# A staged copy issued ahead of a turn instead of behind it, in a depthwise convolution fused with a two-layer network

## The chip, the cores and the metric

The kernel runs on one core of a Trainium2 chip. The core has five engines, each with an instruction queue of its own that it works through in order: TensorE (PE) multiplies matrices into PSUM, VectorE (DVE), ScalarE (ACT) and GpSimd (POOL) work on tiles, and SyncE (SP) here does nothing but start DMAs and pass signals on. Engines wait for each other by semaphores. The metric is the device time of one execution in microseconds (us).

## The reference

Each head h has seven weights, made by a softmax over `weight`. The input `x` (8 sequences of 4096 tokens, 192 channels in 8 heads of 24) is convolved along the sequence with them, and the result goes through two products with a gate between:

```
w = softmax(weight, axis=-1)                      # 8 heads x 7 taps
c[b, s, h, g] = sum_k w[h, k] * x[b, s - 6 + k, h, g]   # zero before a sequence
hid = c @ w_in                                    # 192 -> 2048
y = (hid * cos(hid)) @ w_out                      # 2048 -> 192
```

There are 32,768 tokens. Inputs and output are float32; the kernel multiplies in bfloat16.

## The kernel before

**Tiles and units.** The two products go tile by tile, 512 tokens each, 64 tiles in all. The convolution goes unit by unit, 1024 tokens each, so a unit feeds two tiles: an even one and an odd one. While tiles of unit u are multiplied, the convolved and transposed input of unit u+1 is made ready in a buffer `cT`, of which there are two.

**How a unit is made.** From the fourth unit on (`FIRST_RAW`), part of the tokens is convolved by PE with a band matrix (`conv_unit`, matmuls of L284) and part by ACT and POOL tap by tap on a transposed copy `rT`. Both parts meet in a staging tile `ro`: the first part comes there by two DMA transposes (`turn_unit`, L326), the second by the last of POOL's three additions (`sum_raw`, L393, L394, L396). Then `spread_raw` issues four DMAs from SP that copy the staging tile to both halves of `cT` (L408, L409, twice each). The change is about these four.

**Products.** Product 1 (`mm1`, L524) makes `h` from `cT`, eight steps of a tile, called h0 to h7, each six matmuls; ACT takes its cosine (L531), DVE multiplies (L535). Product 2 (`mm2_step`, L573) uses the `g` of an earlier tile and takes 128 matmuls a tile, in 64 steps of two. The two matmuls of a step work on two halves of PE's rows and write to two banks.

**The turns.** Half way through a tile's product 2 the two row halves change banks. So that no two of them write one bank at once, `Turn` puts an empty instruction on SP (L203) that waits for the last matmuls of the first half (`mark`); the first matmuls of the second half wait for that instruction (`wait`). `conv_unit` has a turn of the same kind between its first eight and its last eight matmuls. So PE goes on past a turn only once SP has come to that empty instruction, and SP comes to it only when it is done with everything that it was given before.

**Order of work.** It is written out by hand as strings. In `PE_ORDER`, one string for even and one for odd tiles, `mN` is N steps of product 2, `hJ` a step of product 1, `q` marks the place of product 2's turn (its empty instruction has been given to SP with the last step ahead of `q`), `c1` and `c2` are the two halves of `conv_unit`, with its turn between. Letters with a number are work on a unit that many ahead: `S` sum_raw, `X` and `x` the transposes to the staging tile, `K` a cast, `R` tap_raw (four multiplications on POOL, L386), `T` the transpose to `rT` (L353), `L` loads, `U` spread_raw; `O` stores results, `p` marks the end of product 2 of a tile. Where an item stands in the string is where its instructions stand in their own engine's queue; an item for SP takes no place on PE. `PE_FIRST` has the strings of the first six tiles.

In the odd tile SP is given: the empty instruction of product 2's turn, the four copies (U+1), the empty instruction of the convolution's turn (c1), the transpose T+3, a store, three loads. In the even tile: the turn of product 2, two transposes X+1 and x+1, a store.

Of the kernel before, what the change touches and what calls it, by code (L numbers as in the profile page):

```python
# [16 lines left out]
def kernel(  # L17
# [14 lines left out]
    T = 512  # L32
# [87 lines left out]
    wo_src = moe_w_out.rearrange("(i j p) d -> p j i d", i=2, p=128)  # L120

    def cast_wo(q):
        have.add(("wo", q))
        nc.gpsimd.tensor_copy(out=wo[:, q * QP : (q + 1) * QP], in_=wo_f[:, q * QP : (q + 1) * QP])  # L124

# [88 lines left out]
    def cast_unit(u, n0=0, n1=UB + 1, copy=nc.gpsimd.tensor_copy):  # L214
        if u >= FIRST_RAW:
            xk[u] = xk_pool.tile([128, NC * (UB + 1), 64], BF16, name="xk")
            for n0, n1 in ((NPB, UB + 1), (0, NPB)):
                copy(out=xk[u][:, NC * n0 : NC * n1].rearrange("p (k n) m -> p k n m", k=NC),  # L218
                     in_=x_tiles[u][:, n0:n1].rearrange("p n (m k) -> p k n m", k=NC))
            if u % UPS == 0:  # L220
                nc.gpsimd.memset(xk[u][0 : 128 - OP, 0 : NC * NPB : NPB], 0.0)
            return
        if n0 == 0:
            bf[u] = xb0 if u == 0 else xbf_pool.tile([128, UB + 1, D], BF16, name="x_bf")
        o = 1 if u == 0 else 0
        copy(out=bf[u][:, n0 + o : n1 + o, :].rearrange("p n (h k r) -> p (n h) k r", k=NC, r=R),  # L226
             in_=x_tiles[u][:, n0:n1, :].rearrange("p n (h r k) -> p (n h) k r", k=NC, r=R))
# [27 lines left out]
    def conv_part(u, c, banks, whole=False):  # L255


        ps = banks()
        nb = UB + 1
        for i in range(4):  # L260
            conv_mm(u, c, ps, i, slice(0, 128), 0, nb, start=i % 2 == 0, stop=i % 2 == 1)
        if u == 1 and c == 0:
            spread_taps(ps[1][:, nb * 2 * G : nb * 2 * G + K])
        yield
        yield
        if u not in ct_tiles:
            ct_tiles[u] = ct_pool.tile([128, UB + 1, NC, 2, 64], BF16, name="ct")
        for b in range(2):
            conv_out(u, c, ps, 0, 0, nb, copies[by[0]], banks=(b,))
            if b and u == 1 and c == 0:  # L270
                nc.scalar.copy(tap, ps[1][:, nb * 2 * G : nb * 2 * G + K])
            if b:
                have.add(("conv", u, c))
            yield

    def conv_unit(u, banks):


        ps = banks()
        sides = [slice(0, 64), slice(64, 128)]  # L280

        def mm(h, side):
            first, last = h % 4 == 0 and h // 4 == side, h % 4 == 3 and h // 4 != side
            return nc.tensor.matmul(  # L284
                out=ps[h // 4][:, 0 : NPB * 4 * G].rearrange("p (m i r) -> p i m r", m=NC * NPB, i=4)[:, h % 4],
                lhsT=band[sides[side], h, 128 - OP : 256 - OP], rhs=xk[u][sides[side], 0 : NC * NPB, R * h : R * (h + 1)],
                start=first, stop=last, skip_group_check=True)

        for h in range(4):
            ms = mm(h, 0), mm(h + 4, 1)  # L290
        turn = Turn()
        turn.mark(*ms)
        yield
        for h in range(4):
            ms = mm(h + 4, 0), mm(h, 1)
            if h == 0:
                turn.wait(*ms)
        yield
        both = ps[0].tensor, ps[0].offset, [ps[0].ap[0][0], OP]
        for n0, n1 in ((1, NPB), (0, 1)):  # L300
            to = ct_bufs[u % 2][0:OP, 2 * NC * min(n0, 1) : 2 * NC * (min(n0, 1) + 1)]
            to = to.rearrange("p (k n) (b w) -> p b k n w", k=NC, b=2)[:, :, :, 0 : n1 - n0]
            nc.scalar.copy(to, bass.AP(both[0], both[1] + 4 * R * n0, [both[2], [T, 2], [NPB * 4 * R, NC], [4 * R, n1 - n0], [1, 4 * R]]))  # L303
            if n0 == 0:
                have.update((("conv", u, 0), ("conv", u, 1)))
            yield
# [75 lines left out]
    def tap_raw(u):  # L382

        p = raw_prod
        for j in range(NG):
            nc.gpsimd.tensor_scalar(out=p[:, j], in0=tap_window(u, PA + j), scalar1=tap[:, PA + j : PA + j + 1],  # L386
                                    scalar2=1.0, op0=ALU.mult, op1=ALU.mult)

    def sum_raw(u):

        assert {("tap", u, j, PARTS[k].start) for j in range(PA) for k in "lr"} <= have
        a, p, add = pa.pop(u), raw_prod, nc.gpsimd.tensor_tensor
        add(out=p[:, 0:PA], in0=p[:, 0:PA], in1=a, op=ALU.add)  # L393
        add(out=p[:, 0:2], in0=p[:, 0:2], in1=p[:, 2:4], op=ALU.add)  # L394
        have.add(("summed", u))
        add(out=stage_of(u)[:, :, NLO * OP : LO], in0=p[:, 0].rearrange("p (k w) t -> p k (w t)", k=NC),  # L396
            in1=p[:, 1].rearrange("p (k w) t -> p k (w t)", k=NC), op=ALU.add)
# [29 lines left out]

    tc.add_manual_dep(nc.sync.nop().ins, summed.ins.name, sync_dep, reason="order of the transfers")
    LOADS = "b l r e | 0 1 2 3"
    for k in LOADS.split("|")[0].split():  # L430
        loads[k]()

    three = {"D": nc.vector.tensor_copy, "A": nc.scalar.copy, "P": nc.gpsimd.tensor_copy}
    for i, k in enumerate("DPDPDPDPDPDPDPAA"):
# [12 lines left out]
    def conv_first():  # L447

        banks = o_banks()
        for half in range(2):  # L450
            for h in range(H):
                for prev in range(2):
                    nc.tensor.matmul(
                        out=banks[half][:, 0 : 2 * D].rearrange("p (n k h r) -> p h n k r", n=2, k=NC, h=H)[:, h],
                        lhsT=band[:, h, 128 * prev : 128 * prev + 128],
                        rhs=bf[0][:, 2 * half + 1 - prev : 2 * half + 3 - prev, h * G : (h + 1) * G].rearrange(
                            "p n (k r) -> p n k r", k=NC),
                        start=(h == 0 and prev == 0), stop=(h == H - 1 and prev == 1), skip_group_check=True)
            m = copies[half](out=ct_tiles[0][:, 2 * half : 2 * half + 2].rearrange("p n k t w -> p (n k) t w"),  # L459
                             in_=banks[half][:, 0 : 2 * D].rearrange("p (m t w) -> p m t w", t=1, w=64).to_broadcast(  # L460
                                 [128, 2 * NC, 2, 64]))
        tc.add_manual_dep(nc.sync.nop().ins, m.ins.name, sync_dep, reason="order of the transfers")
        for k in LOADS.split("|")[1].split():
            loads[k]()

    def turn_first(half):
        for n in range(2):
# [130 lines left out]
    def finish(t):  # L598
        o_sb[t] = opool.tile([128, NB, D], FP32, name="o_sb")
        for si in range(2):  # L600
            for b in range(2):
# [5 lines left out]

    PE_ORDER = ['m11 h0 m3 h1 S+1 m6 h2 m8 q X+1 h3 K+3 m6 h4 m17 h5 x+1 m9 O p h6 h7 m4', 'm11 h0 m5 h1 R+2 m7 h2 m5 q U+1 h3 m8 h4 m6 c1 m12 c2 T+3 h5 m6 O p L+4 h6 h7 m4']  # L610
    ACT_ORDER = ['s0 s1 s2 a0l2 s3 s4 Q a1l4 a1r4 V s5 s6 s7', 'a0r0 s0 s1 s2 s3 a2l3 s4 a2r4 ec1 Q ec2 s5 P s6 s7']

    PE_FIRST = ["K1 k1 h0a h0b W0 W1 h1 h2 h3 r h4 w5 d11 w4 h5 d21 W2 W3 c11 X0 m1 h6 m11 h7 L2 c21 D1",
# [5 lines left out]
    ACT_FIRST = ["s0a s0b s1 s2 er er s3 s4 ed11 ed21 s5 ec11 s6 ec21 s7",  # L619
                "s0 s1 s2 s3 s4 s5 ec12 ec22 Q P s6 ed12 s7 ed22",  # L620
                "s0 s1 s2 s3 Q s4 P s5 s6 s7",
# [11 lines left out]
    for t in range(NT + 1):  # L633
# [34 lines left out]

        def of_unit(k, v):
            if (k, v) == ("K", 1):  # L670
                cast_unit(1, 0, NB)
            elif (k, v) == ("k", 1):
                cast_unit(1, NB)
            elif k == "Z":
                nc.gpsimd.memset(ct_bufs[v][0:OP, 0 : 2 * NC], 0.0)
            elif (k, v) == ("X", 0):
                turn_unit(0, NB, UB)
            elif k == "L":
                load_unit(v)
                if v < FIRST_RAW:  # L680
                    load_edges(v)
            else:
                {"K": cast_unit, "D": double_unit, "X": turn_unit, "Y": mend_edges, "T": turn_raw, "R": tap_raw, "B": more_taps, "S": sum_raw,
                 "U": spread_raw, "x": lambda u: turn_unit(u, part=1)}[k](v)

        for k in pe.split():
# [13 lines left out]
                made = step // (2 * STEPS) - 1  # L700
            elif k == "q":
                assert step % (2 * STEPS) == STEPS
            elif k[0] == "W":
                cast_wo(int(k[1]))
            elif k == "O":
                while stored <= made and (stored, 0) in evacs and (stored, 1) in evacs:
                    store(stored)
                    stored += 1
            elif k[1:] and k[1] != "+":
                of_unit(k[0], int(k[1]))  # L710
            else:
                if u + int(k[2:]) < NU and (k[0] not in "RSUx" or u + int(k[2:]) >= FIRST_RAW):
                    of_unit(k[0], u + int(k[2:]))
# [35 lines left out]
```

## Time and profile before

| | |
|---|---|
| median of three executions | 702.14 us (702.13 to 702.61) |
| the profiled execution's own time | 702.85 us |
| its span, first to last instruction | 700.9 us |
| granted TensorE clock | 0.999 |
| busy share of PE, DVE, ACT, POOL | 99%, 93%, 92%, 82% |

The span leaves out 1.95 us around the instructions. The chain of waits follows the work that ended last back through what released it. In the timeline, a DMA instruction's time is the time that SP is held by it, not that of the transfer. The waits view lists for each engine and line what ended its idle time. PE's weight loads are listed as PEld, beside PE.

### The profile page before, as it was taken

The page shows a single profiled execution, that of the slowest core. Times are in us where ns is not written, and L with a number is a line of the kernel's source. Part 1 is how long each engine was busy: PE and PEld are TensorE (multiplying, and loading weights), DVE is VectorE, ACT ScalarE, POOL GpSimd, SP SyncE. Part 2 cuts the span into 40 slices and gives each one's busy share as a digit, 9 for nine tenths or more (in the row PEclk, how much of TensorE's full clock was granted, in tenths as well). Part 3 has the DMA queues.
Part 4 walks back from the last instruction along what each step waited for, and adds up shares of the span by engine and source line. Part 5 has one row for each costly group of instructions (what it writes and reads, how often), then busy time and mean ns, then how long its engine had stood idle before and what let it go on. Part 6 is the DMA issues. An engine that isn't in the chain of part 4 may idle for free.

```text
span 700.9 us, 26910 instructions
## 1 busy us (share of the span) xinstructions
PE 693.0 (99%) x11838; PEld 505.5 (72%) x11838; DVE 651.1 (93%) x628; ACT 643.4 (92%) x799; POOL 577.3 (82%) x309
## 2 busy tenths in 40 slices
PE   8999999999999999999999999999999999999998
PEld 4677777777776777777777767777777777777776
DVE  6899999999999999999999999999999999999996
ACT  7889999999999999999999999999999999999875
POOL 6698888899888898888898888988888988887600
PEclk9999999999999999999999999999999999999999
DMA  8992666546765457665556654577654466653232
GB/s 211 204 212 70 147 147 142 106 138 148 169 144 124 115 129 170 152 152 94 146 137 169 146 134 110 128 162 162 149 125 117 126 169 161 146 105 84 68 92 69
DMA packets 163133, 95.99 MB, mean 137 GB/s; under 512 B 68808, under 2 KB 162632, under 8 KB 163016
## 3 DMA queue, kind: packets, MB, share of 16 engines
q1 hardware_dynamic: 162304, 93.30, 57.5%
q8 instruction: 92, 1.51, 0.9%
q0 software_dynamic: 416, 0.79, 0.8%
q14 instruction: 25, 0.20, 0.1%
q10 hardware_dynamic: 296, 0.20, 0.1%
HBM read 31.36 MB, written 25.17 MB: 81 GB/s over the span
## 4 chain that ended last, share of the span: by engine, by line
PE 94%; SPq 2%; DVE 1%; ACT 1%; issue 0%; POOL 0%; POOLq 0%
PE h L524 46%; PE o_ps L573 46%; PE h L284 1%; SPq L409 1%; SPq L408 1%; DVE g L535 1%; ACT cs L531 1%; PE h L573 0%; DVE band L436 0%; ACT ct L493 0%; POOL mask L166 0%; PE h L236 0%; ACT mask L171 0%; ACT ct L459 0%; DVE diag L426 0%
## 5 line engine op out<-in xcount | busy, mean ns | idle before, releaser
L535 DVE TENSOR_TENSOR g<-h,cs 128x1024 bf16<-128x1024 f32 (+1 forms) x513 | 597.3, 1217 | 20.7 <-ACT cs L531 12.2
L531 ACT ACTIVATE cs<-h 128x1024 bf16<-128x1024 f32 (+1 forms) x513 | 510.6, 1022 | 45.0 <-PE h L524 37.3
L573 PEld LDWEIGHTS <-g 64*128 64x128 bf16 x8192 | 353.5, 94 | 102.0 <-issue 0.4
L573 PE MATMUL o_ps<-wo,g 64*128 64x192 bf16 x8128 | 413.3, 243 | 0.0
L524 PE MATMUL h<-cT,w 64*128 64x512 bf16 (+1 forms) x3078 | 405.5, 376 | 1.0 <-DVE g L535 0.6
L393 POOL TENSOR_TENSOR raw_prod<-raw_prod,pa 128x3105 f32<-128x3105 f32 x29 | 164.7, 5679 | 64.4 <-ACT pa L377 64.4
L524 PEld LDWEIGHTS <-w 64*128 64x128 bf16 x3078 | 142.9, 94 | 77.6 <-issue 2.4
L386 POOL TENSOR_SCALAR raw_prod<-rT,tap 128x1035 f32<-128x1035 bf16 x116 | 130.5, 1150 | 0.6 <-DMA rT<-xk 0.5
L377 ACT ACTIVATE pa<-rT,tap 128x575 f32<-128x575 bf16 (+1 forms) x168 | 119.0, 728 | 0.0
L394 POOL TENSOR_TENSOR raw_prod<-raw_prod 128x2070 f32<-128x2070 f32 x29 | 111.6, 3847 | 2.3
L218 POOL CAST xk<-x_f 128x1152 bf16<-128x1152 f32 (+1 forms) x58 | 77.8, 1374 | 1.6 <-DMA x_f<-in_x_dram 1.6
L396 POOL TENSOR_TENSOR ro<-raw_prod 128x1035 bf16<-128x1035 f32 x29 | 69.1, 2381 | 2.3
L592 DVE COPY o_sb<-o_ps 128x384 f32<-128x384 f32 x92 | 48.5, 554 | 19.9 <-PE o_ps L573 19.8
L303 ACT CAST ct_buf<-h 112x384 bf16<-112x384 f32 (+1 forms) x58 | 20.2, 401 | 2.0 <-PE h L284 2.0
L284 PE MATMUL h<-xk,band 64*128 64x72 bf16 x464 | 17.1, 194 | 1.8 <-SPq L203 1.8
L592 ACT COPY o_sb<-o_ps 128x384 f32<-128x384 f32 x34 | 16.0, 474 | 0.1
L284 PEld LDWEIGHTS <-band 64*128 64x128 bf16 x464 | 13.8, 95 | 3.0 <-SPq L203 2.9
L226 POOL CAST x_bf<-x_f 128x768 bf16<-128x768 f32 (+2 forms) x4 | 6.4, 1626 | 6.1 <-DMA x_f<-in_x_dram 6.1
L143 PE MATMUL o_ps<-zero 128*128 128x512 bf16 x21 | 7.7, 519 | 1.3 <-DVE zero L138 1.3
L143 PEld LDWEIGHTS <-zero 128*128 128x128 bf16 x24 | 2.4, 117 | 4.5 <-issue 2.6
L124 POOL CAST wo<-g 128x768 bf16<-128x768 f32 x4 | 3.3, 827 | 2.2 <-DMA g<-in_moe_w_out_dram 2.1
L246 ACT CAST ct<-h 128x432 bf16<-128x432 f32 x8 | 4.0, 536 | 0.0
(67 smaller groups left out, 50.1 us busy)
## 6 DMA issues: line engine op xcount, KB each, us to landing
out_dram<-o_sb SPq DMA_DIRECT2D x63, 384.0 KB, 3.2
x_f<-in_x_dram SPq DMA_DIRECT2D x62, 384.0 KB, 5.1
cT<-ro SPq DMA_DIRECT2D x58, 213.4 KB, 3.4
cT<-ro SPq DMA_DIRECT2D x58, 170.6 KB, 4.4
x_f<-in_x_dram SPq DMA_DIRECT2D x31, 96.0 KB, 3.8
g<-in_moe_w_out_dram SPq DMA_DIRECT2D x8, 192.0 KB, 6.0
ro<-ct_buf SPq DMA_TRANSPOSE x58, 2.4
w<-in_moe_w_in_dram POOLq DMA_DIRECT2D x2, 384.0 KB, 6.2
```

The source lines that it names most:

```text
L218: copy(out=xk[u][:, NC * n0 : NC * n1].rearrange("p (k n) m -> p k n m", k=NC), in_=x_tiles[u][:, n0:n1].rearrange("p n (m k) -> p k n m", ...
L284: return nc.tensor.matmul(out=ps[h // 4][:, 0 : NPB * 4 * G].rearrange("p (m i r) -> p i m r", m=NC * NPB, i=4)[:, h % 4], lhsT=band[sides ...
L377: nc.scalar.mul(room_of(u)[:, j, part], tap_window(u, j)[:, part], tap[:, j : j + 1])
L386: nc.gpsimd.tensor_scalar(out=p[:, j], in0=tap_window(u, PA + j), scalar1=tap[:, PA + j : PA + j + 1], scalar2=1.0, op0=ALU.mult, op1=ALU. ...
L393: add(out=p[:, 0:PA], in0=p[:, 0:PA], in1=a, op=ALU.add)
L394: add(out=p[:, 0:2], in0=p[:, 0:2], in1=p[:, 2:4], op=ALU.add)
L396: add(out=stage_of(u)[:, :, NLO * OP : LO], in0=p[:, 0].rearrange("p (k w) t -> p k (w t)", k=NC), in1=p[:, 1].rearrange("p (k w) t -> p k ...
L524: nc.tensor.matmul(out=h[:, i, n0 * 128 : n1 * 128], lhsT=w[rows, k, j, :], rhs=rhs, start=(k == 0), stop=(k == NC - 1))
L531: nc.scalar.activation(out=cs[:, :, part], in_=h[:, :, part], func=AF.Sin, bias=math.pi / 2.0, scale=1.0)
L535: nc.vector.tensor_tensor(out=g_tiles[t][:, 2 * j : 2 * j + 2, part], in0=h[:, :, part], in1=cs[:, :, part], op=ALU.mult)
L573: ms.append(nc.tensor.matmul(out=o_ps[tt, b, si], lhsT=g_tiles[tt][rows, f, s * 128 : (s + 1) * 128], rhs=wo[rows, f // 2, f % 2, :], star ...
L592: (copy or copies[b])(o_sb[t][:, 2 * b : 2 * b + 2, :].rearrange("p s d -> p (s d)"), o_ps.pop((t, b)))
```

## The change

`U+1` moves in the string of the odd tile from behind `q` to the place behind `h0`, in `PE_ORDER` and in the string of the sixth tile in `PE_FIRST`. No instruction is added or removed. On SP, the empty instruction of product 2's turn, which stood ahead of the four copies and their two wait instructions, now stands behind them, in 29 units; the queues of the other four engines keep their order. The diff further adds notes that the program makes while it is built (`have`, `assert`, and `load`, which calls the same loads); they give no instruction. In the changed kernel line numbers are higher by up to 15.

```
-    PE_ORDER = [..., 'm11 h0 m5 h1 R+2 m7 h2 m5 q U+1 h3 m8 h4 m6 c1 m12 c2 T+3 h5 m6 O p L+4 h6 h7 m4']
+    PE_ORDER = [..., 'm11 h0 U+1 m5 h1 R+2 m7 h2 m5 q h3 m8 h4 m6 c1 m12 c2 T+3 h5 m6 O p L+4 h6 h7 m4']
...
-                "m11 h0 m4 h1 R+2 m6 h2 m7 q h3 m5 h4 U+1 m7 c1 m8 c2 m3 h5 T+3 L+4 m9 p O h6 h7 m4"]
+                "m11 h0 U+1 m4 h1 R+2 m6 h2 m7 q h3 m5 h4 m7 c1 m8 c2 m3 h5 T+3 L+4 m9 p O h6 h7 m4"]
...
+    def load(k):
+        have.add(("in", k))
+        loads[k]()
...
     def sum_raw(u):
-        assert {("tap", u, j, PARTS[k].start) for j in range(PA) for k in "lr"} <= have
+        assert {("product", u)} | {("tap", u, j, PARTS[k].start) for j in range(PA) for k in "lr"} <= have
```

More of the change, by code (lines that the diff above doesn't have):

```diff
@@ L122, in cast_wo @@
     def cast_wo(q):
+        assert ("in", str(q)) in have
         have.add(("wo", q))
@@ L224, in cast_unit @@
             bf[u] = xb0 if u == 0 else xbf_pool.tile([128, UB + 1, D], BF16, name="x_bf")
+        if n1 > UB:
+            have.add(("cast", u))
         o = 1 if u == 0 else 0
@@ L255, in conv_part @@
     def conv_part(u, c, banks, whole=False):
+        assert ("cast", u) in have
         ps = banks()
@@ L298, in conv_unit @@
         yield
+        assert ("zero", u % 2) in have
         both = ps[0].tensor, ps[0].offset, [ps[0].ap[0][0], OP]
@@ L384, in tap_raw @@
         p = raw_prod
+        have.add(("product", u))
         for j in range(NG):
@@ L429 @@
     LOADS = "b l r e | 0 1 2 3"
+    def load(k):
+        have.add(("in", k))
+        loads[k]()
     for k in LOADS.split("|")[0].split():
-        loads[k]()
+        load(k)
     three = {"D": nc.vector.tensor_copy, "A": nc.scalar.copy, "P": nc.gpsimd.tensor_copy}
@@ L463, in conv_first @@
         for k in LOADS.split("|")[1].split():
-            loads[k]()
+            load(k)
     def turn_first(half):
@@ L605 @@
     o_ps, o_sb, turns, evacs = {}, {}, {}, set()
-    PE_ORDER = ['m11 h0 m3 h1 S+1 m6 h2 m8 q X+1 h3 K+3 m6 h4 m17 h5 x+1 m9 O p h6 h7 m4', 'm11 h0 m5 h1 R+2 m7 h2 m5 q U+1 h3 m8 h4 m6 c1 m12 c2 T+3 h5 m6 O p L+4 h6 h7 m4']
+    PE_ORDER = ['m11 h0 m3 h1 S+1 m6 h2 m8 q X+1 h3 K+3 m6 h4 m17 h5 x+1 m9 O p h6 h7 m4', 'm11 h0 U+1 m5 h1 R+2 m7 h2 m5 q h3 m8 h4 m6 c1 m12 c2 T+3 h5 m6 O p L+4 h6 h7 m4']
     ACT_ORDER = ['s0 s1 s2 a0l2 s3 s4 Q a1l4 a1r4 V s5 s6 s7', 'a0r0 s0 s1 s2 s3 a2l3 s4 a2r4 ec1 Q ec2 s5 P s6 s7']
@@ L670, in of_unit @@
             if (k, v) == ("K", 1):
+                assert ("in", "l") in have
                 cast_unit(1, 0, NB)
             elif (k, v) == ("k", 1):
+                assert {("in", "r"), ("in", "e")} <= have and 1 in bf
                 cast_unit(1, NB)
             elif k == "Z":
+                have.add(("zero", v))
                 nc.gpsimd.memset(ct_bufs[v][0:OP, 0 : 2 * NC], 0.0)
@@ L702 @@
                 assert step % (2 * STEPS) == STEPS
+            elif k[0] == "I":
+                load(k[1])
             elif k[0] == "W":
```

## The prediction

> **What bounds the kernel now.** The page comes first: who is busy, and what the chain that ended last consists of.
>
> ```profile
> PE 693.0 (99%) x11838; PEld 505.5 (72%) x11838; DVE 651.1 (93%) x628; ACT 643.4 (92%) x799; POOL 577.3 (82%) x309
> ...
> PE 94%; SPq 2%; DVE 1%; ACT 1%; issue 0%; POOL 0%; POOLq 0%
> ```
>
> PE is the bound, and an order on SP doesn't shorten its work. The 2% of SP is some 14 us of chain, yet that isn't what can be won: where the chain runs through SP, PE works beside it for most of the time. What PE itself loses stands in the waits view:
>
> ```profile
> PEld L284 <- SPq L203: 2.9, 5, 0.8
> ...
> SPq L203 <- PE o_ps L573: 305.4, 64, 10.1
> ```
>
> Five times PE's weight loads stood at a convolution (L284) until SP came to a turn's empty instruction (L203), 2.9 us in all, the longest 0.8. The second row is SP's own: it stands at the turns of product 2 for 305 us in 64 waits, and has time to spare. Why it comes late five times is read from SP's timeline and from the chain. First an undisturbed unit, SP and then PE:
>
> ```profile
> 293.51 2.89 SPq L326 DMA_TRANSPOSE ro<-ct_buf  x2
> 296.53 0.50 SPq L595 DMA_DIRECT2D out_dram<-o_sb  x1
> 304.06 0.62 SPq L408 DMA_DIRECT2D cT<-ro  x1
> ...
> 306.02 0.62 SPq L409 DMA_DIRECT2D cT<-ro  x1
> ```
>
> ```profile
> 303.82 0.65 PE h L524 x6
> ...
> 306.27 0.13 PE h L284 x8
> 306.40 0.99 PE o_ps L573 x24
> 307.39 0.13 PE h L284 x8
> ```
>
> Product 2's first half ends at 303.82, where six matmuls of product 1 come between; its second half begins behind them, at 304.47. Only behind that turn do the copies go out, from 304.06, and they hold SP until 306.64. The convolution's first half is done at 306.40, its second starts at 307.39: SP's empty instruction comes there with less than 0.75 us in hand. Then a disturbed unit, by the chain:
>
> ```profile
> 211.97 1.30 PE h L524 x12
> ...
> 218.76 1.79 SPq L409
> ...
> 221.25 0.63 SPq L409
> ...
> 222.00 0.30 PE h L284 x8
> ...
> 223.44 1.30 PE h L524 x12
> ```
>
> One copy holds SP for 1.79 us. The last is through at 221.88, and the convolution's second half starts 0.12 us later: PE was waiting. The 1.17 us that the slow issue adds to an ordinary 0.62 are more than the margin, and PE loses the rest.
>
> **The change, part by part.** *Removed and added:* nothing. *Moved:* on SP, four DMA issues and their two wait instructions change places with one empty instruction. No other queue is touched; POOL, ACT and DVE run what they ran, in the same order.
>
> *What the convolution's turn costs now.* The outer rows of the last fence enclose one stretch with a stall. Here are an undisturbed stretch between the same two points of the order, then the three others that are stalled:
>
> ```profile
> 84.89 1.29 PE h L524 x12
> ...
> 95.61 1.29 PE h L524 x12
> ```
>
> ```profile
> 233.91 1.29 PE h L524 x12
> ...
> 245.12 1.08 PE h L524 x9
> ...
> 382.66 1.30 PE h L524 x12
> ...
> 394.07 1.30 PE h L524 x12
> ...
> 404.54 1.29 PE h L524 x12
> ...
> 415.77 1.29 PE h L524 x11
> ```
>
> Undisturbed: 10.72. Stalled: 11.47, 11.21, 11.41 and 11.23, so 0.75 + 0.49 + 0.69 + 0.51 = 2.44 us. The fifth stall is in the first unit, where the second half's eight matmuls take 0.30 instead of 0.13, hence 0.17. In one more unit a copy took 1.10 and the eight matmuls 0.18, hence 0.05:
>
> ```profile
> 72.49 0.30 PE h L284 x8
> ...
> 560.09 1.10 SPq L409 DMA_DIRECT2D cT<-ro  x1
> ...
> 562.76 0.18 PE h L284 x8
> ```
>
> Sum: 2.44 + 0.17 + 0.05 = 2.66 us, near the 2.9 of the waits view. PE works back to back and nothing makes up for a stall later, so all of it is on the path. After the change only product 2's turn stands directly ahead of the convolution's empty instruction on SP, and that is given 2.4 us before. The stall goes: minus 2.66 us.
>
> *What the new place costs.* The copies wait for POOL's last addition and for the two transposes to the staging tile, and now SP must be through with them when PE needs product 2's turn. POOL's addition in the undisturbed unit, the transposes' time to landing, and the issue times of all copies (least, median, most, in ns):
>
> ```profile
> 296.32 2.38 POOL L396 TENSOR_TENSOR ro<-raw_prod 128x1035 bf16<-128x1035 f32 x1
> ```
>
> ```profile
> ro<-ct_buf SPq DMA_TRANSPOSE x58, 2.4
> ```
>
> ```profile
> L408 SPq DMA_DIRECT2D cT<-ro x58: 595/617/1585, 69.6 to 666.7; - x58
> ...
> L409 SPq DMA_DIRECT2D cT<-ro x58: 594/614/1787, 70.4 to 667.4; - x58
> ```
>
> The sum is there at 298.70. The transposes are issued by 296.40; 2.4 us on, counted from the end of the issue to be safe, is 298.80. SP itself is free from 297.03. With 0.2 for the two wait instructions the copies go out from 299.0. Four at 0.62 with 0.05 between them are 2.6 us: done at 301.6. Product 2's turn can be given at 303.82 and is needed at 304.47, so 2.2 us of cover to the first and 2.9 to the second. The slowest issue recorded, 1.17 us over the ordinary, stays inside. Without cover, every 0.1 us would cost 29 × 0.1 = 2.9 us, since all units have the same order. The bounds: at the low end 0 (a gain is excluded, since PE doesn't wait at product 2's turn now); at the high end all four like the slowest, 4 × 1.79 + 0.15 = 7.3 us, which end at 306.3, 1.8 us late in each of 29 units, 53 us. I take 0, because the medians are 0.62 and 0.61.
>
> *The landing.* The next tile's product 1 reads what the copies write. They land some 5 us earlier; PE doesn't wait there now, so this is worth 0.
>
> *The rest of SP's queue.* The transpose behind the convolution's turn can start when PE is at 306.40, not behind the copies at 306.64, so 0.2 us earlier; the store and loads behind it move with it. Worth 0: PE waits for none of them. What is late next is nothing close. A stretch of a unit's length without a stall, in the columns PE, weight loads, DVE, ACT, POOL:
>
> ```profile
> 262.00:283.20 21.20, 21.20 (x372) 15.61 (x370) 20.17 (x20) 20.13 (x26) 18.82 (x10) 1.00 0.61 140
> ```
>
> PE fills its 21.20 us, DVE and ACT have 1 us left. This is the floor of a unit.
>
> *Sum.* The profiled execution took 702.85 us, span and ends together, 0.71 over the median of 702.14. 702.85 − 2.66 = 700.19 against its own time; 702.14 − 2.66 = 699.48 against the median. I say 699.5.
>
> [...] The row first: a store issued right behind a transpose held SP for 1.62 us.
>
> ```profile
> 306.81 1.79 SPq L353 DMA_TRANSPOSE rT<-xk  x1
> 308.64 1.62 SPq L595 DMA_DIRECT2D out_dram<-o_sb  x1
> ```
>
> A store of the same size behind the two transposes, in the row of 296.53, took 0.50. [...]
>
> **The rivals.** *Slower: the copies' issues stretch at the new place.* Place: product 2's turn, which stands behind them on SP. It decides once four issues that begin at 299.0 end after 304.47, so at over 1.33 us each. At 1.62 each, as in the row above, they end at 305.6 and PE is 1.2 us late in 29 units: 34 us less the 2.7 won, 734 us. For it: the 1.62 row. Against it: the 0.50 of the store that stands directly behind the same two transposes, and that the copies come another 2 us after that store. 5%.
>
> *Half the gain or none: the slow issues belong in part to the profiled execution.* It lies 0.71 us over the median. If that is stalls, ordinary executions have 2.66 − 0.71 = 1.95 us of them and the change gives 700.2; if most of the rest is the profiler's too, it gives 0 to 1.4 us, 700.7 to 702.1. Against it: the slow copies recur at a distance, eight units from 218.76 to the row below and eight more to 560.09, as if they belonged to the program.
>
> ```profile
> 389.45 1.74 SPq L409
> ```
>
> 11% for the part of it that ends within 0.2%.
>
> *The gain of the chain's share.* 2% of 702 us is 14 us: 688 us. Against it: PE waited for 2.9 us alone. 1%.
>
> **How the numbers follow.** The full gain has 83%: 699.5, with a range of its own from 699.0 (the 2.9 of the waits view, and 0.2 of scatter) to 700.4 (1.95 us, and 0.2 of scatter). A measurement of this kernel tells about 0.2% from no change, 1.4 us, so faster means under 700.74. The 83% and the 1% lie there: 84%. Within 0.2%: 11%. Slower: 5%. The range goes from 698.9 up into the second rival, to 701.1; it leaves out the 5% of slower, the 1% for 14 us, and some 7% of the second rival.
>
> **What would show it.** Right: the copies stand in SP's timeline right behind POOL's L396, ahead of product 2's turn by 2 us; PE and its weight loads have no wait at the convolution's turn; the stretches above all take 10.72; slow issues may still occur, with nobody waiting. Wrong: PE or its weight loads wait for SP at product 2 (L573); the copies' issues have a median over 1.3 us; or PE waits for `cT`. A kernel that is faster with the old waits still in place would have its time from something else.

## The result and the profile after

The changed kernel takes 700.14 us in the median of nine executions (699.79 to 700.41), the kernel before 702.14 us in nine beside it (701.53 to 702.85). The ratio is 0.9973, with a 95% interval of 0.9964 to 0.9981: 0.27% faster, 2.0 us. The profiled execution took 699.79 us, its span is 698.0 us.

On the page, the chain that ended last doesn't run through SP any more:

```profile
PE 97%; ACT 1%; DVE 1%; POOL 0%; issue 0%; POOLq 0%
PE o_ps L583 48%; PE h L534 47%; PE h L288 1%; DVE g L545 0%; ACT cs L541 0%; PE h L583 0%; PE o_ps L144 0%; PE h L239 0%; ACT L188 0%; ACT x_bf L229 0%; PE o_ps L463 0%; POOL mask L167 0%; ACT mask L172 0%; ACT ct L469 0%; PE o_ps L496 0%
```

The next rows are all waits of PE's matmuls in the changed kernel (each with the us in all, the number of waits and the longest). L288 is the convolution, L583 product 2, L534 product 1; there is no wait for SP and none for a transfer, and the list of the weight loads has none either:

```profile
PE o_ps L144 <- DVE zero L139: 1.3, 1, 1.3
PE h L534 <- DVE g L545: 0.4, 2, 0.3
PE h L534 <- DVE cT L488: 0.2, 1, 0.2
```

What SP waits for now. The empty instruction (L204) waits for the convolution's first half in each of 29 units, so that SP is there before PE; the first copy (L414) waits for the transposes to the staging tile and for POOL's last addition (L402):

```profile
SPq L204 <- PE o_ps L583: 213.8, 64, 10.1
SPq L204 <- PE h L288: 74.1, 29, 3.0
SPq L414 <- POOL ro L402: 28.3, 25, 1.8
...
SPq L414 <- DMA ro<-ct_buf: 19.8, 28, 2.3
```

SP's timeline over two units, the first with a slow copy:

```profile
297.22 0.61 SPq L414 DMA_DIRECT2D cT<-ro  x1
297.88 0.60 SPq L415 DMA_DIRECT2D cT<-ro  x1
298.53 1.84 SPq L414 DMA_DIRECT2D cT<-ro  x1
300.42 0.61 SPq L415 DMA_DIRECT2D cT<-ro  x1
305.06 2.29 SPq L358 DMA_TRANSPOSE rT<-xk  x1
...
316.64 0.50 SPq L605 DMA_DIRECT2D out_dram<-o_sb  x1
318.40 0.61 SPq L414 DMA_DIRECT2D cT<-ro  x1
...
320.37 0.68 SPq L415 DMA_DIRECT2D cT<-ro  x1
```

And PE in the unit with the slow copy, by the chain; the last row is the place of product 2's turn in the next unit:

```profile
302.31 0.65 PE h L534 x6
302.96 0.66 PE o_ps L583 x16
...
304.76 0.13 PE h L288 x8
304.89 0.99 PE o_ps L583 x24
305.88 0.13 PE h L288 x8
...
323.49 0.65 PE h L534 x6
```

The slow issue is still there, 1.84 us. SP is through at 301.03, product 2's first half ends at 302.31, so the turn waits for nobody. The convolution's first half, the matmuls of product 2 behind it and the second half follow each other without a gap, and the second half takes 0.13 us. In the next unit the copies run from 318.40 to 321.05, 2.4 us ahead of the end of product 2's first half at 323.49, and they start as soon as POOL's sum is there:

```profile
315.99 2.38 POOL L402 TENSOR_TENSOR ro<-raw_prod 128x1035 bf16<-128x1035 f32 x1
```

To compare executions I take the stretch between the same two places of the order, one ahead of the first unit that is staged in this way and one near the end (the first of these rows stands for the kernel before, then two of the changed kernel):

```profile
63.51 1.30 PE h L524 x12
...
669.72 1.29 PE h L524 x12
```

```profile
63.43 1.30 PE h L534 x12
...
666.96 1.29 PE h L534 x12
```

606.21 us before, 603.53 us after, 2.68 us less. The prediction's sum over six units was 2.66. The other 0.4 us by which the two profiled executions differ lies outside the stretch.

### The profile page after: what moved, and what is told of

It is laid out like the page before. It is cut to its first block, busy times and chain, and to the rows that moved or that the text cites. A ratio compares the mean times of both kernels' runs of the same rounds, so it can differ in the third digit from the quotient of the medians.

```text
span 698.0 us, 26908 instructions
## 1 busy us (share of the span) xinstructions
PE 692.3 (99%) x11836; PEld 528.1 (76%) x11838; DVE 650.9 (93%) x628; ACT 642.9 (92%) x799; POOL 577.6 (83%) x309
## 3 DMA queue, kind: packets, MB, share of 16 engines
q8 instruction: 92, 1.51, 1.0%
## 4 chain that ended last, share of the span: by engine, by line
PE 97%; ACT 1%; DVE 1%; POOL 0%; issue 0%; POOLq 0%
PE o_ps L583 48%; PE h L534 47%; PE h L288 1%; DVE g L545 0%; ACT cs L541 0%; PE h L583 0%; PE o_ps L144 0%; PE h L239 0%; ACT L188 0%; ACT x_bf L229 0%; PE o_ps L463 0%; POOL mask L167 0%; ACT mask L172 0%; ACT ct L469 0%; PE o_ps L496 0%
## 5 line engine op out<-in xcount | busy, mean ns | idle before, releaser
L583 PEld LDWEIGHTS <-g 64*128 64x128 bf16 x8192 | 366.8, 94 | 89.2 <-issue 0.4
L583 PE MATMUL o_ps<-wo,g 64*128 64x192 bf16 x8128 | 419.9, 243 | 0.0
L534 PE MATMUL h<-cT,w 64*128 64x512 bf16 (+1 forms) x3078 | 412.2, 376 | 0.7 <-DVE g L545 0.4
L534 PEld LDWEIGHTS <-w 64*128 64x128 bf16 x3078 | 159.1, 94 | 67.8 <-issue 2.2
L402 POOL TENSOR_TENSOR ro<-raw_prod 128x1035 bf16<-128x1035 f32 x29 | 69.1, 2384 | 2.3
L602 DVE COPY o_sb<-o_ps 128x384 f32<-128x384 f32 x92 | 48.5, 554 | 16.5 <-PE o_ps L583 16.4
L288 PE MATMUL h<-xk,band 64*128 64x72 bf16 x464 | 17.9, 194 | 0.0
L288 PEld LDWEIGHTS <-band 64*128 64x128 bf16 x464 | 15.1, 95 | 0.0
L325 POOL COPY ct<-ct 128x1728 bf16<-128x1728 bf16 x2 | 3.3, 1627 | 2.5 <-ACT ct L249 2.5
```

The costliest lines, as they stand in the source:

```text
L288: return nc.tensor.matmul(out=ps[h // 4][:, 0 : NPB * 4 * G].rearrange("p (m i r) -> p i m r", m=NC * NPB, i=4)[:, h % 4], lhsT=band[sides ...
L534: nc.tensor.matmul(out=h[:, i, n0 * 128 : n1 * 128], lhsT=w[rows, k, j, :], rhs=rhs, start=(k == 0), stop=(k == NC - 1))
L583: ms.append(nc.tensor.matmul(out=o_ps[tt, b, si], lhsT=g_tiles[tt][rows, f, s * 128 : (s + 1) * 128], rhs=wo[rows, f // 2, f % 2, :], star ...
L602: (copy or copies[b])(o_sb[t][:, 2 * b : 2 * b + 2, :].rearrange("p s d -> p (s d)"), o_ps.pop((t, b)))
```

## The experiments

The kernel before was timed beside each group: 702.19 us beside the first four (11 executions), 702.31 us beside the last four (13). The strings in the edits are shortened; each edit was also made in the string of the sixth tile.

**Part the copies, without making any of them earlier in time but by an issue.** The theory is that the convolution's turn stood behind too many issues on SP; the rival is that the earlier transfers give the gain.

```
-  U+1 (four copies) ... c1 m12 c2
+  U+1 (first and third copy) ... c1 V+1 (second and fourth copy) m12 c2
```

> The kernel before, with the four copies parted: the first and third (those that the next tile needs) stay behind product 2's turn, the second and fourth go behind the convolution's turn. Theory (the convolution's turn stands behind too many issues on SP): the block ahead of that turn is two issues, 1.3 us shorter, which is more than the 1.17 us that a slow issue adds; no wait of PE or its weight loads at L284, and the whole gain of the change, 700.1 us (699.8 to 700.5). Rival (the gain comes from copies that are made earlier, out of the way of other transfers): two copies stay where they were and two are made later than before, so no gain: 702.1 us.

Measured: 700.04 us (699.96 to 700.29), ratio 0.9972, interval 0.9961 to 0.9983: the whole gain. One unit in SP's timeline, in which a copy was slow (two copies in 1.98 us, not 1.26), and the same unit in the chain:

```profile
556.83 1.98 SPq L408 DMA_DIRECT2D cT<-ro  x2
559.27 1.25 SPq L417 DMA_DIRECT2D cT<-ro  x2
```

```profile
559.05 0.13 PE h L284 x8
559.18 0.99 PE o_ps L581 x24
560.17 0.13 PE h L284 x8
```

SP is free at 558.81, before the convolution's first half is over at 559.18. The second and fourth copy go out only then, later than in the kernel before, and nothing is lost. So the gain is the order on SP, not the time of the transfers: the rival falls.

**Move all copies the other way, behind the convolution's turn.**

```
-  q U+1 h3 m8 h4 m6 c1 m12 c2
+  q h3 m8 h4 m6 c1 U+1 m12 c2
```

> The kernel before, with all four copies moved the other way, behind the convolution's turn. Theory: the stall at that turn is gone as with the change, but the copies start about 2.4 us later than before, the third is issued at about 307.8 in the unit that was shown, lands 3.4 to 4.2 us later, at 311.2 to 312.0, and the next tile's first product step wants it at about 311.0: PE waits for cT 0.2 to 1.0 us in each of 29 units, 706 to 729 us. Rival (all that counts is that no copy stands ahead of a turn): 700.1 us.

Measured: 736.25 us (734.71 to 742.31), ratio 1.0503, interval 1.0467 to 1.0539; 7 us over the top of what was expected. The waits of PE, and a piece of the chain:

```profile
PE h L524 <- DMA cT<-ro: 28.0, 28, 1.7
```

```profile
342.09 0.62 SPq L408
...
342.76 0.60 SPq L409
...
343.40 4.30 DMA cT<-ro
...
347.74 0.69 PE h L524 x5
```

PE waits for the third copy in every unit but one, 1.0 us on average, as much as was expected at most. Against the 700.1 of the changed kernel this one loses 36 us, 28 of them in these waits. The weight loads of product 1, which come ahead of its matmuls, stand idle for 38.0 us (2.4 in the kernel before), which is about the whole; that the 0.3 us a unit between the two is PE starting again is likely and not shown. So a turn that nothing stands ahead of isn't all that counts: the copies have an end to their room on this side too.

**Lengthen SP's block at the old place.**

```
+  def spend(): two DMAs of 128 x 8 elements, ident -> dummy
-  q U+1 h3 m8 h4 m6 c1
+  q U+1 G h3 m8 h4 m6 c1        # G: spend()
```

> The kernel before, with two small DMAs more on SP between the copies and the convolution's turn; they copy 128 x 8 elements from one constant to scratch, and nobody reads them. Theory: SP is held 1.1 us longer (two at about 0.5 and the steps between); the margin at the convolution's turn is 0.43 us (a slow issue of 1.17 us cost 0.75), so PE loses about 0.7 us in each of 29 units, and the slow issues add their full length: 702.1 + 20 + 2, 720 to 727 us, with one wait of PE or its weight loads at L284 per unit. Rival (the turn has more room, and the stalls come from something that happens together with the slow issue): 702.1 us, waits at L284 as few as before.

Measured: 740.61 us (738.28 to 743.50), ratio 1.0543, interval 1.0512 to 1.0573. The waits of the weight loads, and the issue times of the two DMAs (least, median, most, in ns):

```profile
PEld L284 <- SPq L203: 40.2, 28, 2.6
```

```profile
L355 SPq DMA_DIRECT2D dummy<-ident x58: 600/648/1619, 72.5 to 708.3; - x58
```

The mechanism is the expected one, a wait at L284 in 28 of the 29 units, and the rival falls. The size was put too low, for two reasons that the rows show: an added DMA holds SP 0.65 us, not 0.5, which makes it 1.4 us for two, 1.0 us beyond the margin of 0.43 (undisturbed units wait 1.0 to 1.2 us there); and the most, 1.62, shows that they too are slow at times, where now every slow issue counts in full.

**Lengthen SP's block at the new place.** Three and six such DMAs, behind the copies and ahead of product 2's turn.

```
-  m11 h0 U+1 m5 h1
+  m11 h0 U+1 G m5 h1            # spend(): three DMAs; in the second kernel six
```

> The changed kernel, with three small DMAs more on SP (128 x 8 elements from one constant to scratch, which nobody reads) behind the copies and ahead of product 2's turn. Theory: that turn has some 2.8 us of cover behind the copies (2.9 by the chain of the kernel before, less what PE wants earlier); three DMAs at about 0.70 each hold SP 2.1 us longer, so there is no wait of PE or its weight loads for SP in an ordinary unit, and only a unit with a slow issue, 1.2 us more, would lose about 0.5 us: 700.1 to 702.5 us. Rival (the new place has little cover, and is as close to its edge as the old one): 2.1 us more in SP cost over 0.5 us in each of 29 units, over 715 us.

> The changed kernel, with six such small DMAs behind the copies and ahead of product 2's turn. Theory: 4.2 us longer in SP, 1.4 us beyond the cover, so PE or its weight loads wait for SP at product 2 in each of 29 units, some 1.4 us each with 0.2 to start again: 29 x 1.6 = 46 us, 740 to 755 us with slow issues on top. Rival (SP's lateness at product 2's turn isn't passed on to PE): 700 us.

Measured with three: 703.21 us (701.82 to 704.14), 3.1 us over the changed kernel and 0.7 over the expected range; against the kernel before 1.0011 (1.0001 to 1.0021). With six: 750.41 us (749.34 to 755.78), ratio 1.0699 (1.0659 to 1.0738), within the range. The waits of the weight loads with three, then with six:

```profile
PEld L590 <- SPq L204: 3.7, 7, 1.0
```

```profile
PEld L590 <- SPq L204: 58.3, 29, 3.0
```

Three cost something in seven units: in the first one, and in six in which a copy or an added DMA was slow. The profile shows the fastest of the ten executions, 701.82 us; what the others lost beyond it isn't seen. Six cost something in all 29. In the four units of that kernel without a slow issue the block is 4.0 to 4.3 us longer than in the changed kernel, the weight loads wait 1.3 to 1.5 us and the matmuls 0.8 to 1.0. So the cover at the new place is about 2.8 us for the weight loads and 3.2 us for the matmuls, one slow issue takes some 1.2 of it, and past it the wait goes to product 2's turn, as the prediction's first rival has it. That rival's mechanism is real; its condition, long issues in every unit, doesn't come true: the 116 copies of the changed kernel have medians of 0.616 (L414) and 0.610 us (L415) and a most of 2.07.

**Where the slow issues come from.**

```
     keep_warm(9)
+    for _ in range(32):
+        nc.tensor.matmul(out=idle[:, 0:8], lhsT=zero[:, 0:128], rhs=zero[:, 0:8], start=True, stop=True)
```

> The kernel before, with 32 small matmuls more on PE ahead of everything but the warm-up, that is 64 PE instructions with their weight loads. By the page, 92 instruction packets (q8) serve 23,676 PE instructions, 257 each, and a unit has 736, so a packet comes every 7.4 us and its place in the unit moves by some 0.9 us a unit, the same again after eight units. Theory (a copy's issue is slow when such a packet passes at that time): every packet comes 64 instructions, 1.8 us, earlier in the order of work, so that the units with slow copies and stalls come two later: counted from 0, units 9 and 10, 17 and 18, 25 and 26 in place of 7 and 8, 15 and 16, 23 and 24. Rival (slow issues go by SP's own instructions or by the other transfers): the same units as before.

703.19 us in one execution. Units are counted from 0 at the first one that is staged. The copies of units 7 and 9 by SP's timeline (219 and 262 us), then those of 10, 17 and 18:

```profile
220.13 0.60 SPq L411 DMA_DIRECT2D cT<-ro  x1
220.78 0.60 SPq L410 DMA_DIRECT2D cT<-ro  x1
...
262.49 1.23 SPq L411 DMA_DIRECT2D cT<-ro  x1
...
284.50 1.32 SPq L410 DMA_DIRECT2D cT<-ro  x1
...
432.36 1.31 SPq L411 DMA_DIRECT2D cT<-ro  x1
...
454.46 1.35 SPq L410 DMA_DIRECT2D cT<-ro  x1
```

Unit 7, slow in the kernel before, is ordinary here; 9 and 10, 17 and 18 are slow, as are 25 and 26, and, eight units ahead of the first pair, 1 and 2. That is the expected shift by two units, from 64 instructions of PE that moved the work behind them by 0.1 to 0.2 us (the first row of the stretch is at 63.70, against 63.51 to 63.62 in the three traces of the kernel before). SP's own instructions are the same in both kernels, so the rival falls. The units 7, 8, 15, 16, 23 and 24 are the slow ones in all three of these traces. The traces hold the instruction packets too, by queue (packets, MB, share of the 16 DMA engines). The first row is of the four copies of unit 7 in the kernel before (window 218.0 to 221.9), the second of those of unit 9 here (261.8 to 265.1):

```profile
q8 instruction: 1, 0.02, 2.2%
```

```profile
q8 instruction: 1, 0.02, 1.8%
```

Unit 9 of the kernel before (261.7 to 264.4) and unit 7 here (219.4 to 222.1) have no such row. Counting as slow a copy of over 0.8 us, each of the 18 slow copies in the three traces of the kernel before, of the 8 here and of the 4 in the changed kernel has a packet of this queue that starts within it or at most 0.6 us ahead of it. The match has exceptions: with the copies parted, one of seven slow copies has no packet, and in unit 14 of the third trace of the kernel before and in unit 24 here a packet starts among the copies and the longest takes only 0.69 and 0.71 us. Nor is every copy with a packet so close slow: in unit 1 of the kernel before as predicted from, one starts at 93.8, within the fourth copy (from 93.40), which takes 0.60 us, and in its units 14 and 22 and in the units 9 and 25 of the changed kernel one starts up to 0.5 us ahead of the first copy, which takes 0.61 or 0.62. So 36 of these 37 slow copies have such a packet beside them; in what way a packet holds an issue up isn't shown.

**The kernel before, twice more.**

> The kernel before, unchanged, one more execution with its profile. Theory: the time of an execution follows its stalls at the convolution's turn; about 0.7 us less than 702.85 goes with stalls of about 2 us in place of 2.66, and the rest of the span is the same. Rival (the profiled execution differed elsewhere): stalls of 2.66 us again, and the time differs by something else.

> The kernel before, unchanged, a third execution with its profile. Theory: its time less its stalls at the convolution's turn is 699.8 to 700.2 us, as in the two others (702.85 less 2.66, 701.60 less 1.64), and the stalls lie between 1.3 and 2.8 us. Rival: time and stalls don't go together.

The waits of the weight loads at the convolution, in the first and in the second of these executions, and behind each the two rows of the stretch:

```profile
PEld L284 <- SPq L203: 1.8, 5, 0.6
```

```profile
63.52 1.29 PE h L524 x12
...
668.68 1.29 PE h L524 x12
```

```profile
PEld L284 <- SPq L203: 2.3, 6, 0.6
```

```profile
63.62 1.29 PE h L524 x12
...
669.11 1.29 PE h L524 x12
```

| execution | its time | stretch | over 603.53 | time less that |
|---|---|---|---|---|
| kernel before, as predicted from | 702.85 | 606.21 | 2.68 | 700.17 |
| kernel before, again | 701.60 | 605.16 | 1.63 | 699.97 |
| kernel before, again | 702.14 | 605.49 | 1.96 | 700.18 |
| changed kernel | 699.79 | 603.53 | 0 | 699.79 |

Time and stalls go together to 0.2 us. The stalls are no constant of the kernel; three executions have 2.1 us on average, and the medians differ by 2.0.

## Why the prediction was right, and where it was off

*Bound and place.* Right. PE fills its time, and the only place at which the change gains time is the convolution's turn. Parting the copies without the change gives the same 700.0 us.

*What the turn cost.* The mechanism was right, and the sum of 2.66 us was right for the execution that it came from (2.68 by the stretch). The step that was off is the last one, "702.14 − 2.66 = 699.48 against the median". Stalls that change from one execution to the next have to be taken off the time of their own execution, and 702.85 − 2.66 = 700.19 is what the median became, 700.14. The profiled execution was the slowest of the nine, with the most stalls of the three that have a profile. The second rival held this thought, with 1.95 us and 700.2, but laid it to the profiled execution as such; it is the ordinary scatter, since the two further profiled executions had less and took 701.60 and 702.14 us. So the point of 699.5 was 0.6 us low, and the full gain as worked out, with its range up to 700.4, still holds the result.

*What the new place costs.* Right: 0. The block ends 2.4 us ahead of the turn where 2.2 had been worked out, and a slow issue of 1.84 us stays inside. The cover of 2.9 us turned out as 2.8 us for the weight loads and 3.2 us for the matmuls, by the kernel with six DMAs more.

*The landing and SP's other work.* Right: worth 0. Landing two copies later changed nothing either; only 2.4 us later for the third did.

*The rivals.* Slower: its mechanism was seen with six added DMAs, its condition, over 1.33 us for each of the four copies in every unit, isn't met: in the unit of 318.40 they start 1.3 us behind the end of a store's issue and take 0.60 to 0.68 us, and their medians are 0.616 and 0.610 us, against 0.617 and 0.614 in the kernel before. The gain of the chain's share, 14 us: it didn't come, the chain went over to PE nearly whole.

## What to carry to other kernels

An empty instruction that passes a signal through a DMA queue was here only as punctual as the issues ahead of it: two more of 0.65 us each ahead of the convolution's turn made PE's weight loads wait 40.2 us in 28 units. Count the time of the issues, and the slowest of them (1.79 us in the kernel before, where the median was 0.61), against the moment at which the signal is needed. Where work in that queue has room on both sides, put it where nothing that is waited for stands behind it within the time that it takes (here worth 2.0 us), and check both ends of the room, the signal behind it (six added DMAs: 58.3 us of waits) and the reader of the data (the copies behind the convolution's turn: 28.0 us). And take a stall off the time of the execution that shows it, not off a median.

## What was not expected of the hardware

A copy's issue on SP that takes 0.6 us in most units (medians of 0.617 and 0.614 in the kernel before) takes over 0.8 and up to 2.07 us in some. In the three traces of the kernel before these are the units 7, 8, 15, 16, 23 and 24, and they came two units later (9, 10, 17, 18, 25 and 26, with 1 and 2 besides) when PE had 64 instructions more at the start. The page of the kernel before has 92 instruction packets (q8) of together 1.51 MB, 16.4 kB each, and 23,676 instructions of PE with its weight loads, 257 to a packet. That the packets belong to PE's instructions is the author's estimate, from these counts and from the shift; no row says whose they are. PE's own matmuls show no wait that could be theirs: 1.9 us in all in the changed kernel, all for DVE. On SP's queue 36 of the 37 slow copies have a packet beside them, and in the execution predicted from, the stretches with a slow copy hold 2.49 of the 2.66 us that PE lost.
